# Local attention scores as float16 pairs instead of float32, from batch 2 on

## The chip, the cores and the metric

The kernel runs on one core of a Trainium2 chip. The time is that of the device in microseconds (us); the figure for a kernel is the median of its runs. Besides these runs there is one profiled execution, from which all views of the profile come. The engines of the core are called PE (TensorE, the matrix engine, with PEld for its weight loads), DVE (VectorE), ACT (ScalarE), POOL (GpSimd) and SP (SyncE, which issues the transfers).

## What is computed

Attention over 8 batches, 8 heads, 576 positions and 64 dimensions per head, in two branches whose outputs are added, followed by a gated feed-forward layer. In the reference, cut to what matters:

```
q_d, k_d, v_d = means of q, k, v over groups of 4 positions
out_d = softmax(scale * q_d @ k_d.T) @ v_d          # "pooled" branch
out_up = repeat(out_d, 4)
mask = abs(i - j) < 4
scores = where(mask, scale * q @ k.T, -1e9)          # "local" branch
out_local = softmax(scores) @ v
x = (out_up + out_local), heads side by side         # 4608 x 512
out = (sigmoid(x @ w_gate) * (x @ w_val)) @ w_out     # 512 -> 1536 -> 512
```

All inputs and the output are float32. A float16 pair is a number written as a sum of two float16 numbers, a high half and a low half; a product of two pairs is taken as three products (high by high, high by low, low by high).

## The kernel before, in words

**Feed-forward layer.** The 4608 tokens go in 9 chunks of 512 columns, the 1536 inner features in 12 blocks of 128. For each chunk and block PE runs twelve 512-column float16 passes for the gate (`moe_gate`, tile "pg"), twelve for the value (`moe_val`, "pv") and twelve for the output of the block before (`moe_out`, "po"). Between them ACT takes the tanh (L620), DVE multiplies (L628) and ACT and DVE split the product into a pair (L636, L637). "pg" and "pv" have one PSUM bank each, "po" four. The weights come as 64-bit words and are converted in the kernel to float16 pairs, first a pass over all of them for their maxima (`wmax`), then the conversion (`wconv`, L201 to L217): ACT scales a high word (L207), DVE puts the bits together in a tile of tag "wa" (L208 to L210), and ACT, DVE and POOL split it (L158, L159, L216, L217). Tag "wa" has three buffers.

**Attention.** A unit is two heads of one batch: 32 units, four to a batch. `unit_steps` (L413) gives the steps of one: `prep1` copies q into `qblk` (L440), where each of ten blocks of 58 positions stands in a block-diagonal matrix of 128 columns, one head above the other; `qblk` exists twice and its zeros outside the blocks are written once at the start. `s_local` (L461) multiplies each block with its window of 64 keys (tile "s"), in two parts (`s0` with six blocks, `s1` with four), and DVE adds the mask with the scale (L469). Softmax follows (L480 to L491), a transpose (`t_local`, L547, "at"), and the product with v (`av_local`, "x"). For units below 8 (`NPLAIN`, "plain") v and the attention weights stay float32; from unit 8 on they are float16 pairs, v being scaled by a power of two from its maximum over the batch. That maximum is taken by `max_all` (L121): a PE transpose of a column (L127), a maximum by DVE (L129), a diagonal (L131) and a PE product with ones (L132), all in one PSUM bank (tile "mxt"). `pow2` (L141) and `inv_scaled` (L149) make powers of two of it, `split` (L156) writes a pair: the high half by ACT with a scale, the low half by DVE. The pooled branch (`prep2`, `s_down`, `norm_down`, `t_down`, `av_down`; tiles "sd", "adt", "od") runs beside it in float32.

**Queues and order.** The tiles "s", "at", "x", "mxt" and, from unit 4 on, "sd", "adt" and "od" share two PSUM banks (tag "att"). Each step of each unit has a position, base(u) + offset, written out in `T` (L20) and L681 to L768: `run_steps` emits the steps in the order of their positions, between the products of the feed-forward layer, where a position is twelve passes. Units from 8 on follow each other at 6.63 positions (batch 2) and 8.17 positions (later). A framework then schedules the instructions: each engine gets a fixed order, in which an instruction may come ahead of its place when the planner finds the engine free, and waits are put between engines. The q and k of a unit come in one transfer (`load_qk`, L347) into one of two "qk" buffers, which is free again when the unit's scores are done, because the products read k straight from it.

Of the kernel before, what the change touches and what calls it, by code (L numbers as in the profile page):

```python
# [9 lines left out]
F16 = mybir.dt.float16  # L10
F32 = mybir.dt.float32
I32 = mybir.dt.int32
AF = mybir.ActivationFunctionType
ALU = mybir.AluOpType
# [6 lines left out]
P = 128  # L21
# [5 lines left out]
R = 58  # L27
WIN = 64
NBLK = 10
NJ = NBLK // 2  # L30
# [16 lines left out]
NPLAIN = 8  # L47
NKD = 2
QKSCALE = 1.0 / 8
# [9 lines left out]
def attention_moe(ctx, tc, qk, qkd, v, vd, wg, wv, wo, mask, out):  # L59
    nc = tc.nc  # L60

    cp = ctx.enter_context(tc.tile_pool(name="cp", bufs=1))
    raw = ctx.enter_context(tc.tile_pool(name="raw", bufs=2))
    wk = ctx.enter_context(tc.tile_pool(name="wk", bufs=2))
# [16 lines left out]
    mk = cp.tile([P, NJ, 2 * WIN], BF16, tag="mk", name="mk")  # L81
# [27 lines left out]
    qblk = [zeroed(nc.vector, [P, 2 * NJ, P], F32, f"qblk{i}") for i in range(2)]  # L109
# [3 lines left out]
    ad = zeroed(nc.gpsimd, [QM, 2, NKC, 2, WIN], F32, "ad")  # L113
    vblk = cp.tile([P, 2, NBLK, P], F16, tag="vblk", name="vblk")
    flat = {id(vblk): vblk.rearrange("p t b c -> p (t b c)").bitcast(F32)}

    ones = cp.tile([P, 1], F32, tag="ones", name="ones")
    nc.vector.memset(ones, 1.0)
# [22 lines left out]
    def pow2(dst, src):  # L141

        got = max_all(src, src.shape[1])
        nc.vector.tensor_scalar(out=dst, in0=got, scalar1=TINY, scalar2=None, op0=ALU.max)
        nc.vector.tensor_scalar(
            out=dst.bitcast(I32), in0=dst.bitcast(I32), scalar1=EXPBITS, scalar2=None,
            op0=ALU.bitwise_and)

    def inv_scaled(dst, src, c):  # L149
        nc.vector.reciprocal(dst, src)  # L150
        nc.vector.tensor_scalar(out=dst, in0=dst, scalar1=c, scalar2=None, op0=ALU.mult)
# [4 lines left out]
    def split(hi, lo, src, sc):  # L156

        nc.scalar.activation(hi, src, AF.Copy, scale=sc)  # L158
        nc.vector.scalar_tensor_tensor(out=lo, in0=src, scalar=sc, in1=hi, op0=ALU.mult, op1=ALU.subtract)  # L159
# [185 lines left out]
    qkraw, qkdraw, vdraw = {}, {}, {}  # L345
# [44 lines left out]
    HALVES = [slice(0, 64), slice(64, P)]  # L390

    def product(o, w, x, first=True, last=True):

        pairs = ((0, 0), (0, 1), (1, 0)) if len(w) == 2 else ((0, 0),)
        for i, (a, c) in enumerate(pairs):
            nc.tensor.matmul(o, w[a], x[c], start=first and i == 0, stop=last and i == len(pairs) - 1)  # L396
# [4 lines left out]
    def own(t, u):  # L401
        owner[id(t)] = u
# [4 lines left out]
    def zero(*tiles):  # L407

        for t in tiles:
            nc.gpsimd.memset(flat[id(t)], 0.0)  # L410
            own(t, "zero")

    def unit_steps(u):  # L413
        b, hp = divmod(u, NPAIR)
        s = st[u] = {}
        NQ = 2 * NJ * R
        plain = u < NPLAIN
# [9 lines left out]
        QB, VDB = qblk[u % 2], vdblk[u % 2]  # L427
        VB, VT = vblk, vplain[u % 2] if u < NPAIR else vblk
        VBp = [VT] if u < NPAIR else in_parts(vblk, NBLK)

        def take(t):
            if t is vblk and u in (NPAIR, NPLAIN):
                assert owner[id(t)] == "zero", (u, owner[id(t)])
            own(t, u)

        def prep1():
            take(QB)
            q_ = qkraw[u][:, :NQ].rearrange("p (g r) -> p g r", r=R)
            for ps in HALVES:
                nc.scalar.copy(QB[ps, :, ps.start : ps.start + R], q_[ps])  # L440
            s["k"] = qkraw[u][:, NQ:].rearrange("p (a b) -> p a b", b=WIN)

        def plain_v():
            take(VT)
# [16 lines left out]
        def s_local(j0, j1):  # L461
            mine(QB, u)
            n = j1 - j0
            pt = ps_a.tile([P, 512], F32, tag="att", name=f"s_{u}_{j0}")
            for g in range(2 * j0, 2 * j1):
                product(pt[:, (g - 2 * j0) * WIN : (g - 2 * j0 + 1) * WIN], [QB[:, g]], [s["k"][:, g]])
            if j0 == 0:
                s["t"] = wk.tile([P, NJ, 2 * WIN], F32, tag="t", name=f"t_{u}")
            nc.vector.scalar_tensor_tensor(  # L469
                out=s["t"][:, j0:j1, :], in0=pt[:, : n * 2 * WIN].rearrange("p (a b) -> p a b", a=n),  # L470
                scalar=QKSCALE, in1=mk[:, j0:j1, :], op0=ALU.mult, op1=ALU.add)

        def p1():
            s_local(0, 3)
# [113 lines left out]
        def xsplit():  # L588
# [7 lines left out]
            done.add(u)  # L596

        return dict(
            prep0=lambda: None, prep1=prep1, prep2=prep2, s0=p1, s1=p2, sm=p2b,
            d0=lambda: s_down(0), d1=lambda: s_down(1), dn=norm_down,  # L600
            vd=vdsum, v=plain_v if plain else vsplit,
            a0=lambda: t_local(0, 3), a1=lambda: t_local(3, 5), at=t_down, od=av_down,
# [69 lines left out]
    def add(pos, f):  # L672
        steps.setdefault(pos, []).append(f)
# [31 lines left out]
    def base(u):  # L705
        if u < NPAIR:
            return 1 + u * T["pro"]
        if u < 2 * NPAIR:
            return T[f"u{u}"]
        if u < 3 * NPAIR:  # L710
            return C1 - T["b8"] + (u - 2 * NPAIR) * T["s8"]
        return C1 + T["b12"] + (u - 3 * NPAIR) * T["s12"]

    def offset(u, k):
        if u < NPAIR:
            return ALONE[k] * T["al"]
        return AMONG[k] * (T["am"] if u < 2 * NPAIR else 1)
# [29 lines left out]
    worder.sort(key=lambda w: wpos(*w))  # L747
    add(RPOS, ratios)
    add(T["z"], lambda: zero(vblk))
    add(base(NPLAIN - 1) + offset(NPLAIN - 1, "x") + 1, lambda: zero(vblk))  # L750

    for n, (why, k, i) in enumerate(worder):
# [109 lines left out]
```

## Time and profile before

| | us |
|---|---|
| median of 3 runs | 1129.31 |
| lowest, highest | 1126.57, 1129.5 |
| profiled execution | 1126.46 |
| span of its profile (first to last instruction) | 1124.70 |
| PE busy | 1079.2 (96%) |
| DVE busy | 567.7 (50%) |
| ACT busy | 486.7 (43%) |
| POOL busy | 356.7 (32%) |

A row of the profile names the line, the engine, the operation, the tile written and the tiles read with their shapes, and then the busy time or the start and length. Tile names are those of the program without numbers. The line of an instruction can be that of a helper: every product of pairs or of float32 is recorded at L396, so the tile tells which product it is. A float32 product shows as two passes of PE, a product of pairs as three. The busy time of PE is not its price: passes overlap, and ends are modelled.

### The profile page before, as it was taken

The page shows a single profiled execution, that of the slowest core. Times are in us where ns is not written, and L with a number is a line of the kernel's source. Part 1 is how long each engine was busy: PE and PEld are TensorE (multiplying, and loading weights), DVE is VectorE, ACT ScalarE, POOL GpSimd, SP SyncE. Part 2 cuts the span into 40 slices and gives each one's busy share as a digit, 9 for nine tenths or more (in the row PEclk, how much of TensorE's full clock was granted, in tenths as well). Part 3 has the DMA queues.
Part 4 walks back from the last instruction along what each step waited for, and adds up shares of the span by engine and source line. Part 5 has one row for each costly group of instructions (what it writes and reads, how often), then busy time and mean ns, then how long its engine had stood idle before and what let it go on. Part 6 is the DMA issues. An engine that isn't in the chain of part 4 may idle for free.

```text
span 1124.7 us, 15921 instructions
## 1 busy us (share of the span) xinstructions
PE 1079.2 (96%) x6191; PEld 592.0 (53%) x6191; DVE 567.7 (50%) x1050; ACT 486.7 (43%) x1112; POOL 356.7 (32%) x416
## 2 busy tenths in 40 slices
PE   7868878999999999999999999999999999999998
PEld 5753434565555555555555555555555554444443
DVE  7779999854445544444444553544444432112121
ACT  6635666544444444454445443544354332222112
POOL 7435646323323433343333332433243210000000
PEclk8759999999999999999999999999999999999999
DMA  9887766432213222132223121322030000000001
GB/s 368 309 293 276 269 224 197 142 108 80 70 48 126 65 67 70 63 114 71 69 69 108 59 69 56 121 70 66 28 117 14 1 1 38 1 1 38 1 1 38
DMA packets 31899, 110.31 MB, mean 98 GB/s; under 512 B 3536, under 2 KB 3664, under 8 KB 31824
## 3 DMA queue, kind: packets, MB, share of 16 engines
q1 hardware_dynamic: 31824, 109.30, 28.2%
q8 instruction: 49, 0.80, 0.3%
q14 instruction: 26, 0.21, 0.1%
HBM read 99.84 MB, written 9.44 MB: 97 GB/s over the span
## 4 chain that ended last, share of the span: by engine, by line
PE 85%; DVE 8%; ACT 2%; DMA 2%; issue 2%; POOL 1%; DVEq 0%; POOLq 0%; SPq 0%; ACTq 0%
PE po L396 24%; PE pg L396 23%; PE pv L396 23%; PE s L396 5%; PE x L396 3%; PE sd L396 2%; PE od L396 2%; PE at L547 1%; PE adt L557 1%; DVE vdblk L387 1%; DVE hmx L154 1%; DVE wrg L210 1%; DMA wg6c<-in_wg_dram 1%; DVE wrv L209 0%; DVE wrg L209 0%
## 5 line engine op out<-in xcount | busy, mean ns | idle before, releaser
L396 PE MATMUL pg<-xT,wg 128*128 128x512 f16 x1296 | 309.8, 382 | 7.5 <-ACT wg L216 4.3
L396 PE MATMUL pv<-xT,wv 128*128 128x512 f16 x1296 | 310.1, 379 | 3.8 <-DVE tanh L628 3.2
L396 PE MATMUL po<-g,wo 128*128 128x512 f16 x1188 | 280.7, 379 | 0.0
L396 PEld LDWEIGHTS <-wg 128*128 128x128 f16 x1296 | 126.8, 99 | 158.1 <-ACT wg L216 6.9
L396 PEld LDWEIGHTS <-wo 128*128 128x128 f16 x1296 | 126.0, 99 | 149.5 <-ACT wo L158 7.4
L396 PEld LDWEIGHTS <-wv 128*128 128x128 f16 x1296 | 125.5, 98 | 144.0 <-issue 3.1
L628 DVE SCALAR_TENSOR_TENSOR tanh<-tanh,pv 128x512 f32<-128x512 f32 x108 | 73.8, 683 | 195.3 <-PE pv L396 187.6
L620 ACT ACTIVATE tanh<-pg,tsc 128x512 f32<-128x512 f32 (+7 forms) x192 | 86.8, 497 | 153.8 <-PE pg L396 153.3
L636 ACT ACTIVATE g<-tanh,gs 128x512 f16<-128x512 f32 x99 | 71.4, 721 | 149.6 <-DVE tanh L628 148.4
L637 DVE SCALAR_TENSOR_TENSOR g<-tanh,gs,g 128x512 f16<-128x512 f32 x99 | 89.1, 900 | 56.7 <-ACT g L636 56.3
L481 POOL TENSOR_TENSOR t<-t,mx 128x640 f32<-128x640 f32 x32 | 43.9, 1372 | 190.3 <-DVE mx L480 190.3
L396 PEld LDWEIGHTS s<-qk,qblk 128*128 128x128 f32 x600 | 77.0, 196 | 12.3 <-DVE t L469 2.1
L396 PE MATMUL s<-qk,qblk 128*128 128x64 f32 x600 | 76.0, 276 | 4.3 <-DVE t L469 1.5
L594 POOL TENSOR_TENSOR xT<-xs,xT 128x384 f16<-128x384 f32 (+7 forms) x58 | 53.1, 931 | 61.0 <-ACT xT L592 60.2
L491 POOL TENSOR_TENSOR t<-t,sm 128x640 f32<-128x640 f32 x28 | 36.1, 1288 | 89.8 <-DVE sm L489 88.6
L487 DVE TENSOR_REDUCE sm<-t 128x10 f32<-128x640 f32 x32 | 26.1, 817 | 58.3 <-ACT t L482 58.3
L158 ACT ACTIVATE vblk<-v,svb 64x640 f16<-64x640 f32 x48 | 39.6, 825 | 35.4 <-PE x L396 34.0
L440 ACT COPY qblk<-qk 64x580 f32<-64x580 f32 x60 | 40.5, 675 | 24.4 <-DMA qk<-in_qk_dram 17.8
L469 DVE SCALAR_TENSOR_TENSOR t<-s,mk 128x384 f32<-128x384 f32 x64 | 31.1, 486 | 37.6 <-PE s L396 37.4
L513 ACT ACTIVATE mxd<-mxd 72x2 f32<-72x2 f32 x64 | 12.9, 202 | 83.7 <-DVE mxd L512 83.0
L159 DVE SCALAR_TENSOR_TENSOR vblk<-v,svb,vblk 64x640 f16<-64x640 f32 x48 | 46.8, 975 | 4.5 <-ACT vblk L158 2.6
L515 ACT ACTIVATE e<-sd,mxd 72x144 f32<-72x144 f32 x128 | 47.0, 370 | 2.4
(296 smaller groups left out, 1177.7 us busy)
## 6 DMA issues: line engine op xcount, KB each, us to landing
qk<-in_qk_dram SPq DMA_DIRECT2D x30, 610.0 KB, 4.0
qkd<-in_qkd_dram SPq DMA_DIRECT2D x29, 576.0 KB, 3.7
vd<-in_vd_dram SPq DMA_DIRECT2D x29, 384.0 KB, 3.5
v<-in_v_dram SPq DMA_DIRECT2D x32, 320.0 KB, 2.9
out_dram<-osb SPq DMA_DIRECT2D x16, 512.0 KB, 2.9
wo<-in_qk_dram SPq DMA_DIRECT2D x2, 610.0 KB, 9.9
wo<-in_qkd_dram SPq DMA_DIRECT2D x2, 576.0 KB, 9.0
out_dram<-osb SPq DMA_DIRECT2D x4, 256.0 KB, 2.3
```

The lines of the kernel that those rows point to most:

```text
L158: nc.scalar.activation(hi, src, AF.Copy, scale=sc)
L159: nc.vector.scalar_tensor_tensor(out=lo, in0=src, scalar=sc, in1=hi, op0=ALU.mult, op1=ALU.subtract)
L396: nc.tensor.matmul(o, w[a], x[c], start=first and i == 0, stop=last and i == len(pairs) - 1)
L440: nc.scalar.copy(QB[ps, :, ps.start : ps.start + R], q_[ps])
L481: nc.gpsimd.tensor_tensor(out=t, in0=t, in1=mx.unsqueeze(2).to_broadcast([P, NBLK, WIN]), op=ALU.subtract)
L491: eng.tensor_tensor(out=t, in0=t, in1=sm.unsqueeze(2).to_broadcast([P, NBLK, WIN]), op=ALU.mult)
L515: nc.scalar.activation(s["e"][:, qb, h, :], pt[:QM, h * SD : (h + 1) * SD], AF.Exp, bias=mx[:, h : h + 1], scale=QKSCALE / 16, accum_out=s ...
L594: eng.tensor_tensor(out=x[:, hp, 1, o : o + n], in0=src, in1=x[:, hp, 0, o : o + n], op=ALU.subtract)
L620: nc.scalar.activation(t[:, o : o + n], pt[:, o : o + n], AF.Tanh, scale=tsc[:, b, fc : fc + 1])
L628: nc.vector.scalar_tensor_tensor(out=t, in0=t, scalar=1.0, in1=pt, op0=ALU.add, op1=ALU.mult)
L636: nc.scalar.activation(g[:, 0], t, AF.Copy, scale=gs[:, fc : fc + 1])
L637: nc.vector.scalar_tensor_tensor(out=g[:, 1], in0=t, scalar=gs[:, fc : fc + 1], in1=g[:, 0], op0=ALU.mult, op1=ALU.subtract)
```

## The change

For units from 8 on (batches 2 to 7) the local scores are computed with float16 pairs of q and k. A new step `prep0` takes, with ACT's accumulator, the sum of |q| and of |k| along each partition (a bound on the maximum), and one `pow2` over both columns makes a power of two for each; `s2` holds the two scales, `sc` the factor that undoes them. `prep1_16` then splits q (in two halves by partition) and k into pairs. The q pair lies in the same memory as the float32 `qblk` did; the k pair lies in two tiles of tag "wa". Each of the ten products of a unit becomes three float16 passes in place of one float32 product, and the mask step takes its scale from `sc` instead of a constant. Because the pair lies differently in `qblk`, the two tiles are filled with zeros again by POOL after the scores of units 6 and 7. Units 0 to 7 and the pooled scores stay float32. The steps `prep0` stand at the offset -3.14 that `T` already held.

```diff
@@ -113,6 +113,9 @@
+    flat.update({id(t): t.rearrange("p b c -> p (b c)") for t in qblk})
+    sc1 = cp.tile([P, 1], F32, tag="sc1", name="sc1")
+    nc.vector.memset(sc1, QKSCALE * 2.0 ** -26)
@@ -428,17 +431,47 @@
+        QBp = [QB]
+        if not plain:
+            q16 = QB.rearrange("p g c -> p (g c)").bitcast(F16).rearrange("p (t g c) -> p t g c", t=2, c=P)
+            QBp = [q16[:, 0], q16[:, 1]]
...
+        def prep0():
+            t = qkraw[u]
+            s["k16"] = [raw.tile([P, 2 * NJ, WIN], F16, tag="wa", name=f"k16{'hl'[i]}_{u}", bufs=3) for i in range(2)]
+            m2 = wk.tile([P, 2], F32, tag="m2", name=f"m2_{u}")
+            for i, x in enumerate((t[:, :NQ], t[:, NQ:])):
+                junk = s["k16"][i].rearrange("p a b -> p (a b)")
+                nc.scalar.activation(junk[:, : x.shape[1]], x, AF.Abs, accum_out=m2[:, i : i + 1])
+            p2 = wk.tile([P, 2], F32, tag="p2", name=f"p2_{u}")
+            pow2(p2, m2)
+            s["s2"] = wk.tile([P, 2], F32, tag="s2", name=f"s2_{u}")
+            inv_scaled(s["s2"], p2, 2.0 ** 13)
+            s["sc"] = wk.tile([P, 1], F32, tag="sc", name=f"sc_{u}")
+            nc.vector.tensor_scalar(out=s["sc"], in0=sc1, scalar1=p2[:, 0:1], scalar2=p2[:, 1:2], op0=ALU.mult, op1=ALU.mult)
+
+        def prep1_16():
+            own(QB, u)
+            t, s2 = qkraw[u], s["s2"]
+            q_ = t[:, :NQ].rearrange("p (g r) -> p g r", r=R)
+            for ps in HALVES:
+                split(QBp[0][ps, :, ps.start : ps.start + R], QBp[1][ps, :, ps.start : ps.start + R], q_[ps], s2[ps, 0:1])
+            split(*(x.rearrange("p a b -> p (a b)") for x in s["k16"]), t[:, NQ:], s2[:, 1:2])
+            s["k"] = s["k16"]
 
         def prep1():
...
-            s["k"] = qkraw[u][:, NQ:].rearrange("p (a b) -> p a b", b=WIN)
+            s["k"] = [qkraw[u][:, NQ:].rearrange("p (a b) -> p a b", b=WIN)]
@@ -463,12 +496,12 @@
-                product(pt[:, (g - 2 * j0) * WIN : (g - 2 * j0 + 1) * WIN], [QB[:, g]], [s["k"][:, g]])
+                product(pt[:, (g - 2 * j0) * WIN : (g - 2 * j0 + 1) * WIN], [x[:, g] for x in QBp], [x[:, g] for x in s["k"]])
...
-                scalar=QKSCALE, in1=mk[:, j0:j1, :], op0=ALU.mult, op1=ALU.add)
+                scalar=QKSCALE if plain else s["sc"][:, 0:1], in1=mk[:, j0:j1, :], op0=ALU.mult, op1=ALU.add)
@@ -596,7 +629,7 @@
-            prep0=lambda: None, prep1=prep1, prep2=prep2, s0=p1, s1=p2, sm=p2b,
+            prep0=(lambda: None) if plain else prep0, prep1=prep1 if plain else prep1_16, prep2=prep2, s0=p1, s1=p2, sm=p2b,
@@ -747,6 +780,8 @@
+    for u in (NPLAIN - 2, NPLAIN - 1):
+        add(base(u) + offset(u, "s1") + 0.1, lambda u=u: zero(qblk[u % 2]))
```

## The prediction, made blind

> **What bounds the kernel now.** I read the busy time by stretch first, then TensorE's (PE's) instructions in order of time, then the groups of ACT and DVE by form. Columns of the first view: stretch, its length, then busy time and instruction count of PE, PEld, DVE, ACT, POOL, the granted clock, DMA share, GB/s.
>
> ```profile
> 0.00:200.00 200.00, 160.87 (x825) 101.65 (x826) 174.31 (x331) 117.13 (x262) 108.11 (x110) 0.85 0.78 277
> 200.00:900.00 700.00, 698.23 (x4288) 388.82 (x4286) 344.56 (x649) 317.65 (x756) 245.17 (x303) 1.00 0.22 74
> ```
>
> Up to 200 us DVE is busy longest (87%) and PE has gaps. From 200 to 900 us PE is busy for 698.23 of 700 us at full clock, DVE for 49% and ACT for 45%. All that the change touches, units 8 to 31, has its local scores in this second stretch, so there a microsecond taken off PE's stream is a microsecond off the end, and work added to ACT or DVE is free as long as it makes PE wait for nothing. "Busy" overlaps, because matmuls are pipelined, so the price of a group is read from the start of its first instruction to the start of the next group. Columns: start, time to the modelled end, then the group and its count.
>
> ```profile
> 442.25 1.67 PE L396 MATMUL pv<-xT,wv 128*128 128x512 f16 x7
> 443.76 1.45 PE L396 MATMUL s<-qk,qblk 128*128 128x64 f32 x12
> 445.05 0.50 PE L547 MATMUL at<-ident,t 128*128 128x128 f32 x3
> ...
> 449.92 1.00 PE L396 MATMUL s<-qk,qblk 128*128 128x64 f32 x8
> 450.75 0.66 PE L396 MATMUL sd<-kdblk,qks 128*72 128x288 f32 x2
> ...
> 455.35 0.27 PE L127 MATMUL mxt<-ident,vm 128*1 128x128 f32 x1
> 455.46 0.38 PE L396 MATMUL pv<-xT,wv 128*128 128x512 f16 x1
> ...
> 458.48 2.75 PE L396 MATMUL pg<-xT,wg 128*128 128x512 f16 x12
> 461.07 0.59 PE L396 MATMUL pv<-xT,wv 128*128 128x512 f16 x2
> 461.60 0.38 PE L132 MATMUL mxt<-mxg,ones 1*128 1x1 f32 x2
> 461.91 0.39 PE L396 MATMUL pv<-xT,wv 128*128 128x512 f16 x1
> ...
> 472.37 0.98 PE L396 MATMUL x<-at,vblk 128*128 128x58 f16 x30
> 473.18 2.10 PE L396 MATMUL po<-g,wo 128*128 128x512 f16 x9
> ```
>
> **PE: what goes and what comes, per unit.** Removed are the ten float32 score products, which PE runs as 20 passes: 445.05 - 443.76 = 1.29 us for 12 and 450.75 - 449.92 = 0.83 us for 8, together 2.12 us, or 106 ns a pass.
>
> Added are 10 x 3 = 30 float16 passes with 128 columns of weights and 64 moving columns. The trace has their twin in the x product, which already uses pairs: 30 passes with 58 moving columns take 473.18 - 472.37 = 0.81 us, 27 ns each. With 64 columns a pass costs between that (if something other than the columns sets the pace) and 27 x 64/58 = 30 ns. So 0.81 to 0.89 us; I take 0.85.
>
> Also added is one maximum over all partitions (`pow2` through `max_all`), which costs PE a transpose and a float32 product in two passes. The transpose takes 455.46 - 455.35 = 0.11 us. For the product, a 512-column pass is (443.76 - 442.25)/7 = 0.216 us, so the two pv passes begun at 461.07 should have let the next instruction start at 461.50; it was 461.91 when pv went on. That is 0.41 us, and the two together 0.52 us.
>
> Net: 2.12 - 0.85 - 0.52 = 0.75 us less per unit; with 24 units **18.0 us**. By the ends of the pass price it is 17 to 19 us. Note that the maximum eats two fifths of what the faster passes give.
>
> A rule of the Trainium skill speaks against this. "TensorE: Matmul & The Clock Gate", section "Back-to-back issue gap", gives about 81 ns per matmul as the sustained rate of load-and-multiply pairs at 128 columns; by it 30 passes would be 2.43 us, more than the 20 that they replace. The trace doesn't agree: the x row is 27 ns a pass with a new weight load for each.
>
> **ACT, DVE, POOL.** Columns: busy time, mean ns of one, idle time before them.
>
> ```profile
> L440 ACT COPY qblk<-qk 64x580 f32<-64x580 f32 x60 | 40.5, 675 | 24.4 <-DMA qk<-in_qk_dram 17.8 <-DMA wg3m<-in_wg_dram 5.7 <-PE s L396 0.5
> L440 ACT ACT_TABLE_LOAD x1 | 1.3, 1283 | 4.7 <-DMA qk<-in_qk_dram 4.7
> L482 ACT ACTIVATE t<-t 128x640 f32<-128x640 f32 x32 | 23.5, 734 | 19.7 <-POOL t L481 19.4
> L515 ACT ACTIVATION_READ_ACCUMULATOR e<-sd,mxd 72x1 f32 x128 | 24.7, 193 | 0.0
> L158 ACT ACTIVATE vblk<-v,svb 64x640 f16<-64x640 f32 x48 | 39.6, 825 | 35.4 <-PE x L396 34.0
> L159 DVE SCALAR_TENSOR_TENSOR vblk<-v,svb,vblk 64x640 f16<-64x640 f32 x48 | 46.8, 975 | 4.5 <-ACT vblk L158 2.6
> L129 DVE TENSOR_REDUCE mxr<-mxt 1x1 f32<-1x128 f32 x9 | 2.5, 273 | 5.9 <-PE mxt L127 5.9
> L131 DVE TENSOR_SCALAR mxg<-ident,mxr 1x1 f32<-1x1 f32 x9 | 1.8, 196 | 0.1
> L410 POOL MEMSET vblk<- 128x1280 f32 x2 | 2.3, 1162 | 0.0
> ```
>
> ACT loses two copies (1.35 us). It gains two Abs passes with accumulator (2 x (734 + 193) ns = 1.85 us) and three scaled casts (3 x 825 ns = 2.48 us): +2.98 us per unit, 71 us in all. DVE gains three low halves (3 x 975 ns = 2.93 us), the two reductions above (0.47 us) and five one-column operations of under 0.2 us each, by the 196 ns row: at most 4.4 us per unit, 105 us in all. In the 700 us that raises ACT from 45% to 56% and DVE from 49% to 64%. Neither becomes the bound. Head of line: the casts can hold ACT, and the low halves DVE, for 2.5 to 2.9 us at a stretch, and behind them stand the tanh and gate products that free PE's gate and val banks. Such a bank is needed again after two other groups, 2 x (461.07 - 458.48) = 5.2 us, so such a block fits. I price this at nothing; where it collides with the existing v split of the same length, PE would wait a few tenths.
>
> Abs shares no table load with anything seen here: exp, tanh and copy run on the one load of the whole trace. Bounds are 0 and two loads of 1283 ns per unit; even the upper end is 62 us of ACT, 9% of the stretch. I take 0. "ScalarE: Activation LUTs", section "Table sets", of the Trainium skill says that abs is in every set; no run here shows it yet.
>
> **New waits.** PE now needs ACT's sums for the transpose, DVE's diagonal for the product, then ACT and DVE again for the halves. The same round trip is in the trace: from 455.46 to 461.60 PE filled the time with other groups, and lost no more than the 0.09 us contained in the 0.52. In the stretch PE idles for 700 - 698.23 = 1.77 us over 24 units; where it waited for a maximum at the start of the kernel it stood for 2.40 us (the row is under the seam). Bounds: 0, and 24 x 2.40 = 58 us. I take 0, as the stretch's own row is the near one. Two queue effects are free: the q/k tile is released at the split, before the products instead of after them, so SP's load of the next but one unit can only move up; the two POOL fills of `qblk` (2 x 1.16 us) lie after the scores of units 6 and 7, where POOL is idle about half the time.
>
> **The seam at 200 to 235 us.** The halves of k share three buffers ("wa") with the weight conversion. From `T`, unit 8's `prep0` stands at 56 - 6.75 - 3.14 = 46.11; wo 9, 10 and 11 are converted at 44.53, 46.13 and 47.73. So in program order two buffers go to unit 8 just ahead of wo 10, and are held until its scores are done. Whether buffers are handed out in program order shows at the start:
>
> ```profile
> 18.21 1.86 DVE L491 TENSOR_TENSOR t<-t,sm 128x640 f32<-128x640 f32 x1
> ```
> ```profile
> 23.29 1.81 PE L396 MATMUL od<-adt,vdblk 128*128 128x144 f32 x6 [2.28 <-ACT adt L539]
> ...
> 30.14 0.27 PE L127 MATMUL mxt<-ident,vm 128*1 128x128 f32 x1 [2.40 <-DVE vm L304]
> 30.25 0.49 PE L547 MATMUL at<-ident,t 128*128 128x128 f32 x3
> ```
>
> Unit 0's `t` was ready at 20.07 and PE idle, yet its transpose ("at", position 4.32) started only behind the maximum of v (3.83), which takes its bank from the same two; od, of later position (5.40) but another bank, went ahead at 23.29. So a tag's buffers go in program order. Then wo 10 and wo 11 have one buffer between them.
>
> ```profile
> 217.52 0.41 DVE L208 TENSOR_SCALAR wro<-wo11c 128x512 int32<-128x512 int32 x1
> ...
> 222.56 0.80 DVE L159 SCALAR_TENSOR_TENSOR wo<-wro,co,wo 128x512 f16<-128x512 f32 x1 [1.22 <-ACT wo L158]
> ```
> ```profile
> 231.55 2.54 PE L396 MATMUL po<-g,wo 128*128 128x512 f16 x11
> 233.93 2.34 PE L396 MATMUL s<-qk,qblk 128*128 128x64 f32 x20
> ```
>
> One conversion with a buffer of its own takes 223.36 - 217.52 = 5.8 us. Wo 10 would start where wo 11 does now and wo 11 a conversion later, ending near 229.2 us instead of 223.4. Its products run at 231.55, so the cover is 2.4 us thinner than the delay but still there. Bounds: 0, and 5.8 us if the cover is gone; I take 1.5.
>
> **Sum.** The profiled execution took 1126.46 us (span 1124.70 and 1.76 around it). 1126.46 - 18.0 + 1.5 = 1110.0 us. The median of the three runs is 1129.31 (1126.57 to 1129.5), 2.85 above that execution, so on its scale the same sum would be 1112.8. I forecast **1111 us**, between.
>
> **Rivals.**
> - *Round trips stall PE* (chance 0.14). PE takes its instructions in a fixed order, so a late maximum or low half stops it. For: two more crossings per unit each way, and a bank of two held meanwhile. Against: 698.23 of 700. With an eighth to a quarter of the 2.40 us per unit, 7 to 14 us come back: 1118 to 1125 us.
> - *Nothing gained* (0.05). If a pass cost half a float32 pass, 53 ns, 30 take 1.6 us, and 2.12 - 1.6 - 0.52 = 0: 1126 to 1129 us. Against: the x row.
> - *Slower: the weight loads are not hidden* (0.02). One lasts 97 ns:
>
> ```profile
> L396 PEld LDWEIGHTS <-vblk 128*128 128x128 f16 x720 | 23.5, 97 | 6.1 <-issue 0.4
> ```
>
> If each pass cost its load, 30 take 2.9 us, 1.3 us more per unit with the maximum: 31 us more, 1158 us. The 81 ns rule above would act like this. Against: those loads are the x product's own, and it runs at 27 ns.
> - *Slower: buffers go by readiness* (0.07). Unit 8's q was copied 75 us before its scores:
>
> ```profile
> 157.18 1.36 ACT L440 COPY qblk<-qk 64x580 f32<-64x580 f32 x2 [1.00 <-DMA qk<-in_qk_dram]
> ```
>
> If Abs goes there instead and takes two "wa" buffers until 236 us, the 18 conversions still to come (wg and wv 9 to 11, all wo) have one: 18 x 5.8 = 104 us where 66 us (157.18 to 223.36) were used. That is 38 us late, 20 net of the gain: about 1147 us. It decides from a delay of 18 us on. Against: the order of banks above.
>
> **Chances.** The forecast has 0.72 (1105 to 1117 us: pass price, cover of the seam, the 2.85 us between runs), the rivals 0.14, 0.05, 0.02 and 0.07. The range 1104 to 1122 holds the first and part of the second. A measurement of this kernel can tell about 0.3%, 3.4 us: faster than 1125.9 takes the first two, 0.86; same 0.05; slower 0.09.
>
> **What would show it.** Right: groups "s" with f16 and 64 columns, 18 and 12 at 27 to 30 ns; 24 more pairs of "mxt"; PE without gaps from 234 to 885 us; the last x product some 17 us earlier than now; wo 11 finished near 229 us; one table load. Wrong: PE idle ahead of mxt, s or pg in that stretch; passes of over 50 ns; conversions in single file from 157 us; ACT or DVE over 80% there.

## The result, and the profile after

| | before | after |
|---|---|---|
| median, us | 1127.94 (4 runs, 1125.39 to 1129.5) | 1159.16 (4 runs, 1153.09 to 1162.5) |
| span of the profiled execution, us | 1124.7 | 1160.6 |
| PE busy, us (share) | 1079.2 (96%) | 1091.8 (94%) |
| DVE busy, us (share) | 567.7 (50%) | 661.3 (57%) |
| ACT busy, us (share) | 486.7 (43%) | 541.6 (47%) |

The change makes the kernel slower: ratio 1.027, 95% interval 1.0239 to 1.0302. The forecast was 1111 us.

The same two stretches that opened the prediction, now of the kernel after (stretch, its length, busy time and count of PE, PEld, DVE, ACT, POOL, granted clock, DMA share, GB/s):

```profile
0.00:200.00 200.00, 165.06 (x813) 103.36 (x814) 174.81 (x327) 113.10 (x251) 106.06 (x111) 0.81 0.77 270
200.00:900.00 700.00, 670.67 (x4377) 353.38 (x4376) 418.01 (x855) 358.23 (x840) 252.70 (x291) 0.97 0.23 76
```

PE was busy for 698.23 of the 700 us and now is for 670.67, and the clock granted to it fell from 1.00 to 0.97. DVE (60%) and ACT (51%) are not full. So PE waits, and works slower between its waits.

**Where it waits.** Of PE's idle time between 200 and 950 us (29.3 us; before 1.8), 28.0 us lie in five clusters: 351 to 371, 481 to 498, 610 to 625, 734 to 744 and 856 to 864 us. Each is at the start of a chunk of the feed-forward layer. First PE in order of time at such a place before, then at the third cluster after (start, time to the modelled end, group, count, and in brackets the idle time ahead of it with what ended it):

```profile
580.95 0.90 PE L396 MATMUL od<-adt,vdblk 128*128 128x144 f32 x6
581.68 0.38 PE L396 MATMUL pv<-xT,wv 128*128 128x512 f16 x1
581.90 1.89 PE L396 MATMUL po<-g,wo 128*128 128x512 f16 x8
583.62 0.97 PE L396 MATMUL x<-at,vblk 128*128 128x58 f16 x30
584.44 1.02 PE L396 MATMUL po<-g,wo 128*128 128x512 f16 x4
585.30 2.10 PE L396 MATMUL pg<-xT,wg 128*128 128x512 f16 x9
```
```profile
611.93 0.90 PE L399 MATMUL od<-adt,vdblk 128*128 128x144 f32 x6
614.87 1.04 PE L399 MATMUL x<-at,vblk 128*128 128x58 f16 x30 [2.04 <-ACT od L601]
616.49 0.21 PE L399 MATMUL s<-k16h,qblk 128*128 128x64 f16 x1 [0.58 <-DVE xs L619]
...
618.09 0.63 PE L399 MATMUL pg<-xT,wg 128*128 128x512 f16 x1
618.51 0.63 PE L399 MATMUL pv<-xT,wv 128*128 128x512 f16 x1
...
620.78 0.68 PE L399 MATMUL sd<-kdblk,qks 128*72 128x288 f32 x2 [0.99 <-POOL vd L388]
...
622.49 0.59 PE L399 MATMUL pg<-xT,wg 128*128 128x512 f16 x2 [0.81 <-POOL xT L627]
```

Before, feed-forward passes (po, pg, pv) stand between the steps of the last unit of the batch and cover its round trips. After, none is left between od and x: the passes that could run without this unit's x have all been taken, and PE stands still for 2.04 us until ACT has made od. The next chunk needs that x, so attention runs alone, each of its waits in the open.

**Why none is left.** The order of PE is fixed when the kernel is built. The table has the feed-forward passes that stand on PE between the od of one unit and the od of the next, from the last unit of batch 4 on; the first number of a cell is the turn across the chunk start:

| | batch 5 | batch 6 |
|---|---|---|
| before | 95, 110, 109, 132 | 80, 111, 109, 132 |
| after | 36, 118, 129, 149 | 41, 132, 130, 129 |

A turn inside a batch got longer, and more feed-forward work fills it. That work is not new; it is taken out of what should stand at the chunk start, where 36 or 41 passes are left of 95 or 80. PE is full in the long turn and empty at its end. The count isn't the whole of it: the first turn of batch 7 has 71 passes, before 79, and PE still idles for 4.1 us there, most of it (1.61 and 1.25 us) until ACT and DVE have made the halves of k.

**The clock.** Around the same cluster, in stretches of 3.40 us:

```profile
613.00:616.40 3.40, 1.04 (x30) 0.94 (x30) 3.34 (x6) 2.99 (x9) 1.97 (x2) 1.00 0.60 198
616.40:619.80 3.40, 3.30 (x35) 2.53 (x34) 3.26 (x6) 2.36 (x6) 3.37 (x4) 0.50 0.74 266
619.80:623.20 3.40, 1.60 (x8) 0.84 (x8) 2.72 (x7) 2.10 (x7) 3.25 (x6) 1.00 0.34 112
```

After 3.4 us in which PE was busy for 1.04, it gets half its clock for the next 3.4: the two single passes at 618.09 and 618.51 are 0.42 us apart, where a pass is 0.216 at full clock. After chunk 1 began the trace has six stretches at half clock, 44.4 us in all. PE was busy for 37.6 us of them, so at most 18.8 us of work are lost by it. Before had none until its products were done.

**The account.** From the start of chunk 1 (before 236.10, after 234.86) to the last instruction, before and after:

```profile
236.10:1124.70 888.60, 882.25 (x5160) 468.70 (x5159) 364.44 (x673) 353.44 (x821) 236.08 (x294) 1.00 0.17 57
```
```profile
234.86:1160.60 925.74, 892.64 (x5508) 456.03 (x5506) 457.55 (x912) 409.03 (x942) 255.07 (x296) 0.98 0.17 56
```

The stretch is 37.1 us longer. Idle time grows from 6.35 to 33.10: +26.7. Busy time grows by 10.4. The two stretches don't hold quite the same work: the last x of unit 7 (2.17 us) and the scores of unit 8 (0.87 us) lie behind the start of chunk 1 after, and ahead of it before. So the forecast for the stretch is 3.0 - 23 x 0.75 = -14.2; half clock adds at most 18.8, and 5.8 I can't assign. With chunk 1 starting 1.2 us earlier the span is 35.9 us longer. The gain was made and lost more than twice over.

### The profile page after: what moved, and what is told of

It reads as the page before. It is cut to its first block, busy times and chain, and to the rows that moved or that the text cites. A ratio compares the mean times of both kernels' runs of the same rounds, so it can differ in the third digit from the quotient of the medians.

```text
span 1160.6 us, 16930 instructions
## 1 busy us (share of the span) xinstructions
PE 1091.8 (94%) x6503; PEld 577.8 (50%) x6503; DVE 661.3 (57%) x1291; ACT 541.6 (47%) x1232; POOL 373.2 (32%) x418
## 4 chain that ended last, share of the span: by engine, by line
PE 80%; DVE 10%; DMA 3%; ACT 3%; issue 2%; POOL 2%; ACTq 0%; POOLq 0%; DVEq 0%
PE pg L399 23%; PE pv L399 23%; PE po L399 22%; PE s L399 3%; PE x L399 2%; PE sd L399 2%; DMA qk<-in_qk_dram 2%; PE od L399 2%; PE at L580 1%; PE adt L590 1%; PE mxt L135 1%; DVE vdblk L390 1%; DMA qkd<-in_qkd_dram 1%; DVE vm L157 1%; DMA wg6c<-in_wg_dram 1%
## 5 line engine op out<-in xcount | busy, mean ns | idle before, releaser
L399 PE MATMUL pg<-xT,wg 128*128 128x512 f16 x1296 | 324.5, 392 | 14.7 <-ACT wg L219 5.0
L399 PE MATMUL pv<-xT,wv 128*128 128x512 f16 x1296 | 314.6, 384 | 4.5 <-DVE tanh L661 3.4
L670 DVE SCALAR_TENSOR_TENSOR g<-tanh,gs,g 128x512 f16<-128x512 f32 x99 | 79.1, 799 | 44.7 <-ACT g L669 44.3
L390 POOL TENSOR_TENSOR qks<-qkd 128x144 f32<-128x144 f32 x29 | 16.9, 583 | 167.0 <-PE sd L399 166.8
L162 DVE SCALAR_TENSOR_TENSOR vblk<-v,svb,vblk 64x640 f16<-64x640 f32 x48 | 53.9, 1122 | 2.7 <-ACT vblk L161 0.8
L388 POOL TENSOR_TENSOR qkd<-qkd 128x576 f32<-128x576 f32 x29 | 37.9, 1307 | 53.5 <-DMA qkd<-in_qkd_dram 53.5
L161 ACT ACTIVATE vblk<-v,svb 64x640 f16<-64x640 f32 x48 | 39.6, 824 | 22.7 <-PE x L399 22.1
L399 PE MATMUL sd<-kdblk,qks 128*72 128x288 f32 x128 | 45.7, 447 | 4.2 <-DVE at L574 1.5
L502 DVE SCALAR_TENSOR_TENSOR t<-s,sc,mk 128x384 f32<-128x384 f32 (+1 forms) x48 | 26.1, 546 | 39.0 <-PE s L399 38.8
L162 DVE SCALAR_TENSOR_TENSOR qblk<-qk,s,qblk 64x580 f16<-64x580 f32 x48 | 39.9, 832 | 12.1 <-ACT qblk L161 11.3
L157 DVE TENSOR_REDUCE vm<-v 128x1 f32<-128x640 f32 x32 | 26.1, 815 | 34.1 <-DMA v<-in_v_dram 33.8
```

The source lines that it names most:

```text
L157: nc.vector.tensor_reduce(dst, src, axis=AX.X, op=ALU.max, apply_absolute_value=True)
L388: nc.gpsimd.tensor_tensor(out=x[:, :, 0:2], in0=x[:, :, 0:2], in1=x[:, :, 2:4], op=ALU.add)
L670: nc.vector.scalar_tensor_tensor(out=g[:, 1], in0=t, scalar=gs[:, fc : fc + 1], in1=g[:, 0], op0=ALU.mult, op1=ALU.subtract)
```

## The experiments

Four theories were put to the test. **A**: the three "wa" buffers tie unit to unit (Abs of the next unit waits for the scores of this one; its group stood idle for 21.9 us behind s). **B**: the maximum's trip, ACT to PE to DVE to PE to DVE, holds one of the two attention banks, which are handed out in order, and so stretches the turn of a unit. **C**: the load on ACT and DVE. **D**, added later: the trip costs the same wherever its columns lie. Medians, with the ratio to before and its interval:

| run | what differs | us | ratio |
|---|---|---|---|
| e1_stage | k pair in an idle buffer | 1167.07 | 1.0357 (1.0315 to 1.0398) |
| e2_const | no maxima | 1108.66 | 0.9833 (0.9799 to 0.9867) |
| e3_absmax | maximum by DVE, not ACT | 1163.37 | 1.0321 (1.0264 to 1.0379) |
| e4_maxonly | before, with unused maxima | 1187.25 | 1.0518 (1.0481 to 1.0554) |
| e5_batch | one maximum a batch | 1128.49 | 1.0007 (0.9989 to 1.0025) |
| e6_guest | trip earlier, no bank of its own | 1127.02 | 0.9991 (0.9971 to 1.001) |
| e7_two | trip in two banks | 1174.91 | 1.0406 (1.0376 to 1.0436) |
| e8_shift | e6, units 1.5 steps earlier | 1126.47 | 0.998 (0.9959 to 1.0001) |
| e9_bguest | e5 and e6 together | 1122.63 | 0.995 (0.9931 to 0.9968) |
| e10_bgshift | e9, units 1.5 steps earlier | 1124.89 | 0.9965 (0.9947 to 0.9984) |
| e11_beforeshift | before, units 1.5 steps earlier | 1128.87 | 1.0019 (1.0 to 1.0039) |
| e12_early | e1, trip earlier | 1146.14 | 1.0159 (1.0141 to 1.0177) |
| e13_lateguest | e1, no bank of its own, trip later | 1170.92 | 1.0377 (1.035 to 1.0404) |

### e1_stage: another place for the k pair

```diff
-            s["k16"] = [raw.tile([P, 2 * NJ, WIN], F16, tag="wa", name=f"k16{'hl'[i]}_{u}", bufs=3) for i in range(2)]
+            kk = raw.tile([P, 2, 2 * NJ, WIN], F16, tag="stage", name=f"k16_{u}", bufs=NST)
+            s["k16"] = [kk[:, 0], kk[:, 1]]
```

> The k pair lies in one tile of the idle weight-load tag (five buffers) instead of two of the three conversion buffers; nothing else differs from the changed kernel. Theory A (the sums of |k| of a unit must wait for the buffers that the unit before holds until its scores, so each unit starts a chain behind the last): the scores come 28 to 29 us apart again instead of 32, PE has no gaps at the chunk starts, and the time is 1108 to 1116 us. Theory B (the maximum's round trip through PE and DVE holds one of the two attention banks and stretches the chain of units, whatever the buffers): units stay 31 to 33 us apart and the time stays at 1145 to 1162 us. Theory C (ACT and DVE are too loaded, every hop is longer): as B, nothing changes by more than 5 us.

1167.07 us (1165.27 to 1173.34), 8 us more than the change, which no run explains. PE idles 34.7 us at the chunk starts. Theory A falls: the sums of |k| no longer wait for the scores of the unit before (the 21.9 us are gone), and no time is won.

### e2_const: no maxima

```diff
-            m2 = wk.tile([P, 2], F32, tag="m2", name=f"m2_{u}")
-            for i, x in enumerate((t[:, :NQ], t[:, NQ:])):
...
-            pow2(p2, m2)
+            p2 = p2c
```

> Leaves out the maxima: both powers of two are the constant 256, so the Abs sums, the transpose, the product with ones and their DVE steps are gone; the pairs, the three passes and the shared buffers stay. Without them PE has 24 x 0.52 = 12.5 us less to do than the change. Theory A and theory B both: no late units, 1126.5 - 24 x (2.12 - 0.85) = 1096 us, up to 1102. Theory C: ACT loses only 1.85 of its 2.98 us more and DVE 1.2 of 4.1, so units still lag, over 1115 us.

1108.66 us (1106.85 to 1112.21), 18.4 less than before and 50.5 less than the change, but 7 us above what was expected. In its profile chunk 1 starts at 244.55 us, 8.5 later than before; the first 200 us ran at a lower clock (0.68 and 0.90 in the first two hundreds, against 0.76 and 0.94), which may account for it. From there to the end:

```profile
244.55:1110.40 865.85, 855.20 (x5394) 436.81 (x5390) 429.39 (x805) 372.77 (x843) 233.37 (x294) 1.00 0.18 59
```

That is 22.7 us less than the 888.60 of before, at full clock, with the pairs, their splits and all waits for them in place; by the passes alone it should be 23 x (2.12 - 0.85) = 29.2 less (the scores of unit 8 lie ahead of the stretch in both). Of the 6.5 that are missing, 4.3 are idle time (10.65 against 6.35). Between od and od stand 104, 106, 116, 126 and 95, 106, 111, 128 feed-forward passes, as even as before. The pairs are not what costs; the maximum is.

### e3_absmax: the maximum by DVE

```diff
-                junk = s["k16"][i].rearrange("p a b -> p (a b)")
-                nc.scalar.activation(junk[:, : x.shape[1]], x, AF.Abs, accum_out=m2[:, i : i + 1])
+                absmax(m2[:, i : i + 1], x)
```

> The maximum of |q| and |k| is taken by DVE (no scratch output), so only the split needs the shared buffers, not the maximum; DVE has 24 x 1.6 = 38 us more, ACT 45 us less. Theory A: most of the loss goes, 1108 to 1122 us. Theory B: the round trip is still there, 1145 to 1165 us. Theory C: DVE is loaded more, 1150 us or more.

1163.37 us (1158.47 to 1169.71). Two Abs passes and their reads went from ACT to DVE and nothing was won. This alone doesn't decide between B and C, whose ranges overlap here. Theory C, the load, expected over 1115 us for e2_const, where 1108.66 came, and falls by that.

### e4_maxonly: the maximum alone

The kernel before, to which the sums and `pow2` of units 8 to 31 are added, with scratch in an idle buffer and the powers unused; the scores stay float32.

```diff
+        def prep0():
+            t = qkraw[u]
...
+                nc.scalar.activation(junk[:, : x.shape[1]], x, AF.Abs, accum_out=m2[:, i : i + 1])
+            p2 = wk.tile([P, 2], F32, tag="p2", name=f"p2_{u}")
+            pow2(p2, m2)
```

> The kernel before with float32 scores, to which only the sums of |q| and |k| and the round trip of the maximum are added (scratch in the idle weight-load tag, result unused; no pairs, no split). Theory A: only PE's own price shows, 1126.5 + 24 x 0.52 = 1139 us (1136 to 1143). Theory B: the round trip holds the bank here too and late units stall PE at the chunk starts: 1155 us or more. Theory C: little load is added, 1136 to 1143 us.

1187.25 us (1182.81 to 1188.16): the maximum costs 60 us with nothing waiting for its result, where PE's own part is 24 x 0.52 = 12.5. Theory C expected 1136 to 1143 and falls here too. Nothing waits for the scales, so such a loss doesn't need scores that wait for their pairs. What is left is what the trip holds and what stands behind its instructions.

### e5_batch: one maximum for four units

```diff
+            t = raw.tile([P, WPC * 2], F32, tag="stage", name=f"qkm{u}_{i}", bufs=NST)[:, : c.stop - c.start]
+            nc.sync.dma_start(t, qk[u][:, c])
+            nc.scalar.activation(t, t, AF.Abs, accum_out=qkm[b][:, i, hp : hp + 1])
...
+            nc.vector.tensor_reduce(m2, qkm[b], axis=AX.X, op=ALU.max)
+            pow2(qkp[b], m2)
```

> One pair of powers for the four units of a batch in place of one for each: q and k of a batch are loaded a second time into the idle stage tiles ahead of it, their sums of absolute values are made there, and one maximum for a batch (6 in place of 24) goes over PE and DVE. The scores stay float16 pairs. Theory B: a quarter of the round trips is left, and they lie ahead of a batch where no unit waits for them: 1108.7 of constant powers + 6 x 0.52 = 3.1 to a quarter of the loss of 50 more: 1110 to 1124. Theory C (the load on ACT and DVE) and a rival of added traffic (24 x 0.62 MB more through the queues): 1140 or more.

1128.49 us (1125.81 to 1133.01): 31 less than the change, but 4.5 above the range. PE idles 23.6 us, of it 4.7 at 354 to 363 us, where the maximum of v and the steps around it stand in the start of chunk 2. The trips that are left still stand in banks of their own.

### e6_guest: the trip earlier, in columns of other banks

The transpose of unit u's sums is put into the first score bank of unit u-1, the product into its second:

```diff
+            if u in guest:
+                m2, later = guest[u]
+                if j0 == 0:
+                    nc.tensor.transpose(pt[:2, 384:512], m2, ident)
+                else:
+                    nc.tensor.matmul(pt[:, 256:258], ones[:2, :].to_broadcast([2, P]), s["dg"], start=True, stop=True)
```

> Same result as the changed kernel, with the pair of k in one stage tile as in e1_stage. From unit 9 on the maximum takes no attention bank of its own: the transpose of unit u's sums goes into columns 384 to 511 of the first score bank of unit u-1, the product with ones into columns 256 and 257 of its second score bank, and the sums of absolute values are made just before that first bank. All of the maximum's work stays (transposes and products on PE, about 0.52 us a unit, the sums on ACT, five small operations on DVE). Theory B (the maximum's bank, held for some 5 us among banks handed out in program order, stretches the chain of a unit): units 28 to 30 us apart, no late xT at the chunk starts, half clock after 205 us under 10 us, and a time between that of constant powers, 1108.7 us, and that plus 24 x 0.52 = 12.5 us: 1109 to 1121. Rival D (any trip from ACT over PE and DVE back to the scales costs as much, wherever its columns lie): 1150 or more, like e1_stage's 1167.

1127.02 us (1123.93 to 1131.51), 40 less than e1_stage with the same work, and 6 above the range. Theory D expected 1150 or more and falls as it was put. PE in order of time, kernel e6_guest:

```profile
507.59 0.69 PE L399 MATMUL s<-k,qblk 128*128 128x64 f16 x18
508.11 0.27 PE L511 MATMUL s<-ident,m 128*2 128x128 f32 x1
...
513.30 0.51 PE L399 MATMUL s<-k,qblk 128*128 128x64 f16 x12
513.74 0.38 PE L513 MATMUL s<-mxg,ones 2*128 2x2 f32 x2
```

From transpose to product the trip takes longer than in the change (median 5.6 us against 4.0), but it has no bank of its own, and it starts 28 us ahead of its unit's scores, not 20 (medians). Feed-forward passes between od and od are 64, 93, 112, 136 and 102, 111, 115, 133. From chunk 1 to the end:

```profile
230.90:1124.20 893.30, 875.99 (x5508) 451.54 (x5506) 449.43 (x912) 405.40 (x939) 243.51 (x296) 0.99 0.18 58
```

The stretch holds the same extra work as that of the change. Busy 6.3 us less than before (-14.2 by the forecast, at most +5.6 for 13.7 us at half clock, 2.3 over), idle 11.0 more. So most of the forecast gain is there, and gaps at the chunk starts with the clock behind them take it back: the median is that of before (1127.08).

### e7_two: the trip in two banks

```diff
+        pt = ps_a.tile([P, 512], F32, tag="att", name=uniq("mxp"))
         nc.tensor.matmul(pt[:, 256 : 256 + n], ones[:n, :].to_broadcast([n, P]), dg, start=True, stop=True)
```

> The changed kernel with one difference: the product with ones goes into a second attention bank, so that the bank of the transpose is free as soon as its maximum is read. One bank held for some 5 us becomes two held for 1 to 2 us each, but they are two users in the order of banks, not one. Theory B with the length of the hold as the cause: 1130 to 1150. Theory B with the place in the order as the cause (each user waits for the one two before it, however short it is): 1155 to 1185, no better or worse than the change's 1159.

1174.91 us (1174.02 to 1175.94). That is inside the range given for the place in the order as the cause. A shorter hold for each is worth nothing when it is bought with one more user of the two banks; 16 us were added.

### e8_shift, e9_bguest, e10_bgshift, e11_beforeshift: the rest of the gaps

The shift is `s8=6.63` to `s8=6.13` and `b12=26.05` to `b12=24.55` in `T`. e9_bguest is e5_batch with the guest columns of e6_guest.

> e6_guest with the attention units of batches 2 to 7 put earlier among the steps of the feed-forward part: the spacing of units 8 to 11 is 6.13 steps in place of 6.63, the start of batch 3 is 24.55 in place of 26.05, so that units 11 to 31 stand 1.5 steps earlier. All work is the same. In e6_guest PE still idles 11.9 us between 200 and 950 us, nearly all at the chunk starts, where the last unit of a batch comes too late, and then runs 13.7 us at half clock (6.8 lost). Theory B (lateness at the chunk starts is all that is left of the loss): 18.7 us less, 1108 to 1114. Rival (the order of the schedule matters little, the idle time comes from the trip over DVE and ACT itself): 1122 to 1130.

> e5_batch (one pair of powers a batch) with the maximum of batches 3 to 7 put into the unused columns of the score banks of the last unit of the batch before, as in e6_guest, and its sums 8 steps earlier; batch 2 keeps a bank of its own. In e5_batch the trip of the batch's maximum stood in the gaps at the chunk starts (23.5 us idle in all, of it 5 waiting for the maximum's own operations). Theory B: the gaps at the chunk starts shrink to those of constant powers (7.8 us): 1109 to 1118. Rival D (second loads and the sums on ACT cost it, not the bank): 1123 to 1130, as e5_batch.

> e9_bguest with units 11 to 31 1.5 steps earlier, as in e8_shift. Theory B with lateness at the chunk starts: PE idle under 5 us and no half clock after 250 us, 1103 to 1111, the shortest of all. Rival: within 4 us of e9_bguest.

> The kernel before (float32 scores, no maxima) with units 11 to 31 1.5 steps earlier, the control for e8_shift and e10_bgshift. Its PE idles only 1.7 us between 200 and 950 us, so there is nothing to win: 1125 to 1130 by theory B; if the earlier place helps by itself, under 1122.

Measured: e8_shift 1126.47 us (1122.06 to 1130.62), e9_bguest 1122.63 (1119.89 to 1124.44), e10_bgshift 1124.89 (1122.25 to 1128.44), e11_beforeshift 1128.87 (1127.05 to 1134.81). The shift wins nothing in three kernels (-0.6, +2.3 and +1.2 us): e8_shift still idles 12.4 us, half of it at 346 to 363 us. That the rest of the gaps goes away when attention stands 1.5 steps earlier in the program is refuted. Joining e5 and e6 gains 6 us over e5, short of the range. e9_bguest and its shifted form e10 are the kernels with maxima that beat the kernel before, by half a per cent at most: ratio 0.995, interval 0.9931 to 0.9968, for e9.

### e12_early and e13_lateguest: place or bank

e6_guest changed two things at once. e12_early has its place in the order with a bank of its own; e13_lateguest has guest columns in the bank of unit u-1's second pooled scores, and was meant to be about as late as e1; its steps are moved to fit that bank.

```diff
+            at = p0 + offset(u, k)
+            if k == "prep0" and u > NPLAIN:
+                at = base(u - 1) + offset(u - 1, "s0") - 0.1
```
```diff
+            if qb == 1 and u in guest:
+                nc.tensor.transpose(pt[:2, 384:512], m2, ident)
...
+                nc.tensor.matmul(pt[:, 300:302], ones[:2, :].to_broadcast([2, P]), dg, start=True, stop=True)
...
+            if u > NPLAIN and k in ("prep0", "prep1"):
+                d1 = base(u - 1) + offset(u - 1, "d1")
+                at = min(at, d1 - 0.1) if k == "prep0" else max(at, d1 + 0.05)
```

> e1_stage (k pair in a stage tile, the maximum in an attention bank of its own) with the sums and the maximum of unit u at the place in the order that e6_guest gives them, just before the first scores of unit u-1. e6_guest differs from e1_stage in two things, the bank and this place; this run has the place alone. Theory B (the bank counts): 1155 to 1175, near e1_stage's 1167. Rival (the earlier place counts, because the scales are ready in time): 1122 to 1135, near e6_guest's 1127.

> e1_stage with one difference: from unit 9 on the maximum takes no bank of its own, and its trip starts no earlier than the change starts it. The transpose of unit u's sums and the product with ones go into unused columns (384 to 511, and 300 and 301) of the second downsampled-score bank of unit u-1, the attention user nearest to the change's place for the trip; that bank is held longer by the trip. With e1_stage (own bank, late: 1167.1), e12_early (own bank, early: 1146.1) and e6_guest (no bank, early: 1127.0) it is the fourth of two by two. Theory B, additive (the bank costs 19, the late place 21, whichever the other is): 1143 to 1152. Bank alone where late (the early place only hides it): 1122 to 1135. Rival (a late trip costs the same in any bank, since the bank that it lies in is held as long): 1158 to 1172.

| median, us | bank of its own | columns of another's bank |
|---|---|---|
| late | 1167.07 (e1) | 1170.92 (e13, later still) |
| early | 1146.14 (e12) | 1127.02 (e6) |
| no trip | 1108.66 (e2) | |

Neither answer of e12 came: 1146 lies between the two. e13 came inside the range of its rival, that a late trip costs the same in any bank. With a bank of its own the earlier place saves 21 us; early, guest columns save 19 more. The late row compares less well. Transpose, product and first scores of a unit, e1_stage and then e13_lateguest:

```profile
779.98 0.27 PE L130 MATMUL mxt<-ident,m 128*2 128x128 f32 x1
...
784.47 0.38 PE L135 MATMUL mxt<-mxg,ones 2*128 2x2 f32 x2
...
800.88 0.69 PE L399 MATMUL s<-k,qblk 128*128 128x64 f16 x18
```
```profile
772.05 0.27 PE L561 MATMUL sd<-ident,m 128*2 128x128 f32 x1
...
776.81 0.38 PE L566 MATMUL sd<-mxg,ones 2*128 2x2 f32 x2
...
785.04 0.19 PE L399 MATMUL s<-k,qblk 128*128 128x64 f16 x1
```

The trip starts 20.9 us ahead of its scores in e1 and 13.0 in e13 (medians of all units 20.1 and 10.1). So e13's trip is later as well as a guest, and it isn't shown that guest columns save nothing at e1's place. In the early row the place can't be what saves the 19 us: e12's trip is the earlier one (35.4 us ahead, e6's 28.2). But e6 also puts the product behind the second scores, away from the transpose. PE from 350 to 950 us, before, e13_lateguest, e12_early and e6_guest:

```profile
350.00:950.00 600.00, 598.23 (x3692) 329.25 (x3691) 274.84 (x519) 268.42 (x642) 202.14 (x250) 1.00 0.20 67
```
```profile
350.00:950.00 600.00, 571.85 (x3745) 300.01 (x3744) 349.67 (x712) 301.42 (x708) 210.65 (x259) 0.95 0.21 67
```
```profile
350.00:950.00 600.00, 573.59 (x3887) 302.83 (x3886) 346.88 (x710) 306.69 (x721) 201.97 (x258) 0.98 0.20 66
```
```profile
350.00:950.00 600.00, 589.09 (x3953) 312.50 (x3953) 339.57 (x710) 304.84 (x726) 207.45 (x251) 0.99 0.20 66
```

Theory B is right that the trip costs, and too narrow in naming the bank alone. In e13 the bank that lends its columns is held across the trip all the same; in e6 the trip is spread over two banks that were to be used anyway, and neither is held from transpose to product. What stays open: which wait of the late trip sets the pace. The bank is one way, the instructions queued behind the trip's own on ACT and DVE are another, and no run here takes the second away alone.

## Why the prediction was wrong, point by point

**PE bounds the kernel: right, and misread.** 698.23 of 700 us busy was read as if work put on PE were the only price there. It only says that, in the kernel before, every wait of attention was covered by feed-forward passes, and those are a stock: a chunk has 432 of them, and the next chunk's need the last unit of the batch.

**Price of the passes: right.** 18 passes of s, first and last, and the next group, kernel after:

```profile
766.59 0.19 PE L399 MATMUL s<-k16h,qblk 128*128 128x64 f16 x1
...
767.08 0.19 PE L399 MATMUL s<-k16h,qblk 128*128 128x64 f16 x1
767.11 0.53 PE L580 MATMUL at<-ident,t 128*128 128x128 f32 x3
```

0.52 us for 18, 29 ns each (27 to 30 forecast); the 12 of s1 run from 772.65 to 773.00, 29 ns. The rule of the Trainium skill weighed there ("TensorE: Matmul & The Clock Gate", section "Back-to-back issue gap", about 81 ns) is for 128 moving columns; carried over to the 64 of these rows, as the prediction weighed it, it does not hold. The rivals "nothing gained" and "weight loads not hidden" fall with it; that the time came near the 1158 of the second is chance.

**ACT, DVE and the table: right.** Groups of the kernel after (busy time, mean ns, idle time before):

```profile
L452 ACT ACTIVATE k16l<-qk 128x640 f16<-128x640 f32 x24 | 17.7, 736 | 23.2 <-PE s L399 21.9 <-DVE wo L162 1.3
L161 ACT ACTIVATE k16h<-qk,s 128x640 f16<-128x640 f32 x24 | 19.9, 828 | 0.6
L162 DVE SCALAR_TENSOR_TENSOR k16l<-qk,s,k16h 128x640 f16<-128x640 f32 x24 | 23.2, 966 | 0.6
L473 ACT ACT_TABLE_LOAD x1 | 1.3, 1283 | 4.7 <-DMA qk<-in_qk_dram 4.7
```

736, 828 and 966 ns for 734, 825 and 975, and one table load in all, as the Trainium skill's rule in the prediction has it ("ScalarE: Activation LUTs", section "Table sets"). DVE is at 60% (64 forecast), ACT at 51% (56).

**The seam: the order right, the size not.** ACT and DVE there, kernel after:

```profile
211.79 0.68 ACT L452 ACTIVATE k16h<-qk 128x580 f16<-128x580 f32 x1
...
213.82 0.74 ACT L452 ACTIVATE k16l<-qk 128x640 f16<-128x640 f32 x1 [1.25 <-DVE wo L162]
```
```profile
224.27 0.75 DVE L162 SCALAR_TENSOR_TENSOR wo<-wro,co,wo 128x512 f16<-128x512 f32 x1 [0.18 <-ACT wo L161]
```

Abs of unit 8 stands among the last conversions, not 75 us ahead of them, so the rival "buffers by readiness" falls. wo 11 ends at 225.0, where 229.2 was forecast: its conversion began at 221.60 and took 3.4 us, not 5.8. Whether 1.5 us were lost can't be read from the start of chunk 1: it came 1.2 us earlier, but with 3.0 us of attention still to do, and the first 200 us had another clock (0.81, before 0.85).

**New waits: this is the step that failed.** It said "Bounds: 0, and 24 x 2.40 = 58 us. I take 0, as the stretch's own row is the near one." The trip costs 50.5 us (the change against e2), or 60 (e4 against before), 12.5 of it PE's own work. The row that was called near, 455.46 to 461.60, shows a trip for the maximum of v, once a batch; one for each of the four units of a batch is part of the pace. The step asked whether PE finds other groups to fill the time. It does, and that is where the cost sits: one turn of the kernel after, from PE, DVE and ACT,

```profile
772.65 0.19 PE L399 MATMUL s<-k16h,qblk 128*128 128x64 f16 x1
...
778.27 0.38 PE L580 MATMUL at<-ident,t 128*128 128x128 f32 x2
778.49 1.03 PE L399 MATMUL pv<-xT,wv 128*128 128x512 f16 x4
779.35 0.27 PE L130 MATMUL mxt<-ident,m 128*2 128x128 f32 x1
...
783.85 0.38 PE L135 MATMUL mxt<-mxg,ones 2*128 2x2 f32 x2
```
```profile
784.26 0.16 DVE L147 TENSOR_SCALAR p<-mxt 128x2 f32<-128x2 f32 x1 [1.45 <-PE mxt L135]
```
```profile
785.11 1.58 ACT L161 ACTIVATE qblk<-qk,s 64x580 f16<-64x580 f32 x2
```

has no gap, and still the bank is held from 779.35 to 784.4, and the second pooled scores, whose exps stand behind the splits on ACT, come at 788.50. Scores of successive units start 33 us apart (766.59, 800.25, 833.22), before 29 (734.88, 764.21, 793.32). Over these two turns that is 8.2 us, and the chunk start pays.

**The rivals.** "Round trips stall PE" had the right place, and was priced at an eighth to a quarter of 2.40 us a unit, 7 to 14 us, with a chance of 0.14. It even named the bank held meanwhile. But it priced the wait of PE at the trip, and neither the delay handed on to the chunk start nor the clock: of the 51 us lost, 26.7 are gaps and up to 18.8 work at half clock, which no part of the prediction had.

## What to carry to other kernels

An engine that is 99.8% busy hides a new round trip only as long as there is filler, and filler is a stock: before pricing a wait at nothing, find the next point where the stock runs out (here the chunk that needs the last unit) and add up the delay to there, once per unit. A cross-partition maximum inside a software pipeline should be taken a turn earlier and in space that is held anyway; the same work cost 58, 37 or 18 us here by place and bank (e1, e12 and e6 against e2, whose k pair lies in another buffer). Where a matrix engine's gaps come in clusters, price the clock behind them as well: here up to 18.8 us for 26.7 of gaps.

## What the runs showed of the hardware

A gap need not be long to halve the clock. No single gap of the kernel after in these clusters is longer than 2.8 us, but in 3.40 us with 1.04 us of work the clock for the next 3.4 fell to 0.50; the stretches at half clock in its record are 3.41, 6.83 and 20.48 us long, whole multiples of 3.41. At half clock the f16 score passes started 50 to 55 ns apart instead of 29. The Trainium skill ("TensorE: Matmul & The Clock Gate", section "What's actually happening") has the free-running window of 3.4 us, which these lengths agree with, and calls for one idle window; the rows here show a window that was busy for a third. Ahead of the six stretches PE was busy for 0.59, 2.15, 1.86, 1.04, 1.51 and 1.02 us of 3.41. Cut into windows of 3.41 us that end where such stretches begin, the 15 traces of this case (from 240 us on, without the last 40) have 29 windows at full clock with PE busy for less than 1.43 us, and half clock follows each. It follows 24 of the 72 between 1.43 and 2.31 us, and none of the 3566 above.
